# Forward transform: the buffers of its two products and the engine of a 33-row subtraction

## The chip, the cores and the metric

The kernel runs on one core of a Trainium2 chip. A core has TensorE (matrix products into PSUM; PE in the profile, PEld for its weight loads), VectorE (DVE), ScalarE (ACT), GpSimd (POOL) and the queue of SyncE (SP), which issues most transfers. PSUM has eight banks of 512 fp32 values per partition; a product lands in one of them and has to be copied out before the bank can be used again. GpSimd also issues some transfers from its own queue. The metric is the device time of one execution in microseconds (us).

## The reference, cut to what matters

Two independent parts are computed and set side by side. Part A is attention with a compressive memory (32 heads, four segments of 512 positions, projections, output projection). Part B, which the change touches, is a spectral filter:

```python
def _B_ref(x, w_r, w_i):                 # x: 1 x 2048 x 576
    B, S, D = x.shape
    X = jnp.fft.rfft2(x, axes=(-2, -1))  # 2048 x 289, complex
    X = X * (w_r + 1j * w_i)
    return jnp.fft.irfft2(X, s=(S, D), axes=(-2, -1))
...
return jnp.concatenate([a, b], axis=-1)
```

## The kernel before, in words

Part B's forward transform comes first, and the projections of part A follow it. The 2048 rows are split into 16 units of 128 rows. For each unit the transform along the 576 columns is a first product (`f1`) with a table of cosines and sines, and the transform along the 128 rows a second one (`c1`) with a table of its own for each unit (`cfw`). What is left along the 16 units, butterflies and twiddles, is done in place on `Z` (`stage1`, `middle`, `last`), spread over later work by a counter (`pace`) that lets a set number of VectorE instructions go ahead at each place.

fp32 accuracy is had from a fast matmul type by splitting each operand into a rounded high part and the rest (`h` and `l`), and adding three products. So each unit goes through these steps:

- `load`: 384 KB `xin` on SyncE's queue, three buffers.
- `prep`: VectorE makes the sum and the difference of the two mirrored halves (`eo`, two buffers, L125); ScalarE rounds them into `eh` (L127, three buffers); VectorE subtracts to get `el` (L131), and for the rows beyond 256, which lie in partitions 64 to 96 of the third block, subtracts in place in `eh` (L132, 33 rows). Units 0 and 1 do this in halves.
- `f1`: 14 matmuls, seven for the real and seven for the imaginary half, into one PSUM tile of two banks (three such buffers). The seventh of each half reads the 33 rows of L132.
- `ev0` and `ev1`: ScalarE copies the result rounded (`X0`, L146), VectorE subtracts for the rest (`X1`, L149).
- `c1`: 12 matmuls, six for each half, into a one-bank tile for each half (two such buffers).
- `evz`: ScalarE copies either half into `Z` (L153).
- `loadc`: the unit's `cfw` table, issued on GpSimd's queue, four buffers.

The loop over `u` (20 turns) writes the order out by hand, and every engine works its queue in that order: `ev0` of unit u-1, `evz` of unit u-4, the first half of `prep` of unit u+2, `ev1` of unit u-1, one paced step, the second half of `prep`, `f1` of unit u, `load` of unit u+4, `c1` of unit u-3, `loadc` of unit u+1, and one step of splitting part A's weights (`wqkl`, L406 and L407 on VectorE). In the last turns the inputs of the projections are loaded and split instead (L427 to L439). The projections' matmuls are those of L460.

GpSimd has little to do in this stage: a few memsets, three issues for the tables and the sixteen `cfw` issues. Its first subtraction or sum of two tensors is much later, at L532.

Of the kernel before, what the change touches and what calls it, by code (L numbers as in the profile page):

```python
# [5 lines left out]
F32=mybir.dt.float32; F32R=mybir.dt.float32r  # L6
# [96 lines left out]
class FFT:  # L103
# [4 lines left out]
    def forward(s,xp,cp,pp,wl,xs,consts):  # L108

        nc,io=s.nc,s.io; v=nc.vector  # L110
        xin={}; cw={}; C={}; eh={}; el={}; F={}; X={}
        def load(u):
            xin[u]=xp.tile([128,2,3,128],F32,name="xin",bufs=3)
            nc.sync.dma_start(xin[u],io["xb"][u])
        def loadc(u):
            a,b=BORD[u]
            cw[u]=cp.tile([128,2,384],F32R,name="cfw",bufs=4)
            nc.gpsimd.dma_start(cw[u],io["cfw"][4*a+b].rearrange("p (h m) -> p h m",h=2))
        def prep(u,halves=False):

            x=xin.pop(u)
            eo=xp.tile([128,2,3,128],F32,name="eo",bufs=2)
            h=xp.tile([128,2,3,128],F32R,name="eh",bufs=3)
            for r,op in enumerate((OP.add,OP.subtract)):
                v.tensor_tensor(eo[:,r],x[:,0],x[:,1],op=op)  # L125
                if halves: nc.scalar.copy(h[:,r],eo[:,r])
            if not halves: nc.scalar.copy(h,eo)  # L127
            yield
            l=xp.tile([128,2,2,128],F32R,name="el",bufs=3)
            for w in (slice(0,1),slice(1,2)) if halves else (slice(0,2),):  # L130
                v.tensor_tensor(l[:,w],eo[:,w,:2],h[:,w,:2].bitcast(F32),op=OP.subtract)  # L131
                v.tensor_tensor(h[64:97,w,2],eo[64:97,w,2],h[64:97,w,2].bitcast(F32),op=OP.subtract)  # L132
            eh[u],el[u]=h,l
            yield
        def f1(u):
            p=pp.tile([128,2,512],F32,name="f1",tag="f1")
            h,l=eh.pop(u),el.pop(u)
            for r in range(2):
                L=[(h[:,r,0],tab[:,0,r,0]),(h[:,r,1],tab[:,0,r,1]),(h[:,r,0],tab[:,1,r,0]),(h[:,r,1],tab[:,1,r,1]),
                   (l[:,r,0],tab[:,0,r,0]),(l[:,r,1],tab[:,0,r,1]),(h[:99,r,2],tab2[:99,r])]  # L140
                for n,(x,t) in enumerate(L):
                    nc.tensor.matmul(p[:,r,:FP],x,t,start=n==0,stop=n==6)  # L142
            F[u]=p
        def ev0(u):
            x=xp.tile([128,2,FP],F32R,name="X0",bufs=3); X[u]=[x]
            nc.scalar.copy(x,F[u][:,:,:FP])  # L146
        def ev1(u):
            x=xp.tile([128,2,FP],F32R,name="X1",bufs=3)
            v.tensor_tensor(x,F.pop(u)[:,:,:FP],X[u][0].bitcast(F32),op=OP.subtract)  # L149
            X[u].append(x)  # L150
        def evz(u):
            a,b=BORD[u]
            for r,p in enumerate(C.pop(u)): nc.scalar.copy(s.Z[:,b,a,r],p[:,:FP])  # L153
        def c1(u):
            a,b=BORD[u]; x=X.pop(u); cc=cw.pop(u)
            for r in range(2):
                p=pp.tile([128,512],F32,name="c1",tag="c1")
                n=0
                for (i,hl) in ((0,0),(0,1),(1,0)):
                    for q in range(2):  # L160
                        k=(0 if q==0 else 2) if r==0 else (1 if q==0 else 0)
                        nc.tensor.matmul(p[:,:FP],cc[:,hl,k*128:(k+1)*128],x[i][:,q],start=n==0,stop=n==5)
                        n+=1
                C.setdefault(u,[]).append(p)
        load(0)
        tab=cp.tile([128,2,2,2,FP],F32R,name="ftab",bufs=1)
        tab2=cp.tile([128,2,FP],F32R,name="ftab2",bufs=1)
        nc.gpsimd.dma_start(tab[:,0],io["ftab"][:,:4*FP].rearrange("p (r c f) -> p r c f",r=2,c=2))
        late=consts()
        nc.gpsimd.dma_start(tab[:,1],io["ftab"][:,4*FP:].rearrange("p (r c f) -> p r c f",r=2,c=2))  # L170
        nc.gpsimd.dma_start(tab2,io["ftab2"].rearrange("p (r f) -> p r f",r=2))
        load(1); load(2); late()
        for u in range(2): loadc(u)
        p=[prep(u,True) for u in range(2)]
        for i in range(2):
            for x in p: next(x)
        load(3)
        s.pace=Pace(61+165+40)
        for u in range(20):
            p=prep(u+2) if u+2<16 else iter(())  # L180
            if 0<u<17: ev0(u-1)
            if 3<u: evz(u-4)
            if u%4==3 and u>6: s.pace.add(s.stage1((u-7)//4))
            next(p,None)
            if 0<u<17: ev1(u-1)
            if u<14: s.pace.take(1)
            next(p,None)
            if u<16: f1(u)
            if u+4<16: load(u+4)
            elif u<18: next(xs,None)  # L190
            if 2<u<19: c1(u-3)
            if 0<u<15: loadc(u+1)
            if 1<u: next(wl,None)
            if u>13: s.pace.take(2)
        for _ in wl: pass
        for _ in xs: pass
# [188 lines left out]
class ATT:  # L385
# [11 lines left out]
    def consts(s):  # L397
        nc,io=s.nc,s.io
        for i in range(1,4): nc.gpsimd.memset(s.zst[i],0.0)
        return lambda: (nc.sync.dma_start(s.ident,io["ident"]),nc.sync.dma_start(s.bm,io["bm"].rearrange("p (h c) -> p h c",h=7)))  # L400
# [642 lines left out]
def emit(nc,tc,io):  # L1043
    def pool(es,name,bufs=1,**kw):
        return es.enter_context(tc.tile_pool(name=name,bufs=bufs,reuse_waits="tile",**kw))
    with ExitStack() as L0:
        cp=pool(L0,"cp"); dp=pool(L0,"dp",space=bass.MemoryType.DRAM)
        A=ATT(nc,tc,io,cp,dp)
        Rz=ExitStack(); Rv=ExitStack(); Rw=ExitStack(); Ri=ExitStack(); L1x=ExitStack()
        tc.swap_default_side()  # L1050
        zp=pool(Rz,"z"); ftp=pool(Rz,"ft")
        wq=pool(Rw,"wq")
        tc.swap_default_side()
        A.wh,A.wl={},{}
        F=FFT(nc,tc,io,zp); F.tp=A.ftp=ftp
        with tc.manual_schedule():
            x0=pool(L1x,"x0")
            with ExitStack() as es:
                xp=pool(es,"xf",2); cf=pool(es,"cf"); st=pool(es,"st",2)
                pf=es.enter_context(PP(tc,"pf",dict(f1=3,c1=2)))  # L1060
                F.forward(xp,cf,pf,A.load_w("wqk",1152,wq,st,576,"wst",3),A.first(Slots(x0),xp),A.consts)
            with ExitStack() as es:
                wv=pool(Rv,"wv"); xp=pool(es,"xp"); tp=pool(es,"tp",2); fwp=pool(es,"fw",2)
                pp=es.enter_context(PP(tc,"pp",dict(pj=5,pt=1,pm=2)))
                F.pace.add(F.middle(fwp)); F.pace.add(F.last())
                def hook(g,i):
                    if g==3 and i==9:
                        Rw.close()
                        tc.swap_default_side()
                        F.yp=pool(Ri,"yp",2); F.Yt={}; ci=pool(Ri,"ci")  # L1070
                        tc.swap_default_side()
                        F.inv_setup(ci)
                    if g==3 and i>10: F.ysplit(i-11,nc.vector)
                    if g==3 and i==0: q0.extend(A.stacks0(x0))
                    if g==3 and i==3: A.masks()
                    if g==3 and 0<i<7:
                        for _ in range(2): q0.pop(0)()
                q0=[]
                A.projections(xp,tp,pp,wv,F.pace,hook)
            Rv.close()  # L1080
            with ExitStack() as L1:
                cp2=pool(L1,"cp2"); sm=pool(L1,"sm",2); sp=pool(L1,"sp",3)
                ps1=L1.enter_context(PP(tc,"ps1",dict(s1=3)))
                A.begin(sm,sp,ps1)
                with ExitStack() as es:
                    pi=es.enter_context(PP(tc,"pi",dict(i2=2,i3=2,mt=1)))
                    yl=pool(es,"yl",2)
                    A.att_setup(cp2)
                    A.psm,A.mtag=pi,"mt"
                    pr=A.prologue(); next(pr)  # L1090
                    for i,_ in enumerate(F.inverse(yl,pi)):
                        if i>7 and i%4!=3: next(pr,None)
                    for _ in pr: pass
                Ri.close(); Rz.close()
                with ExitStack() as es:
                    tp=pool(es,"tp2",2); ps=es.enter_context(PP(tc,"ps",dict(s2=3,pv=1,post=1)))
                    A.attention(tp,ps)
            L1x.close()
# [18 lines left out]
```

## Time and profile before

| | us |
|---|---|
| median of three runs (725.75 to 726.9) | 725.89 |
| span of the profiled execution, first to last instruction | 725.3 |
| TensorE busy in the span | 693.1 |
| VectorE busy | 551.2 |
| ScalarE busy | 455.1 |
| GpSimd busy | 209.4 |
| first matmul of the forward transform | 8.55 |
| first matmul of the projections | 75.40 |

No other time than the span is given for the profiled execution; the median of the runs lies 0.6 us above it. The granted TensorE clock is 0.999 of full speed over the whole span.

Rows that begin with two numbers are from the order of time: start and duration in us, engine, line, operation, output and inputs with their shapes, count, and in brackets the idle time before and what ended it. Consecutive instructions of the same form are merged into one row; matmuls overlap, so their durations are longer than the distance of their starts. Rows with a bar are groups: count, busy time in us and mean in ns, then the idle time before them. Rows that begin with a stretch (40.00:50.00) give its length, then the busy time and count of TensorE, its weight loads, VectorE, ScalarE and GpSimd, the granted clock, the share of the DMA engines and GB/s. A `q` behind an engine's name marks its instruction queue.

### The profile page before, as it was taken

Reading aid. Unit: us, or ns where it says so; the run is one execution under the profiler, and the core shown is the slowest. Engines: PE = TensorE matmul, PEld = TensorE weight load, DVE = VectorE, ACT = ScalarE, POOL = GpSimd, SP = SyncE. Lnnn points to the kernel's source line nnn. Section 1 sums busy time; section 2 is a strip of 40 time slices with the busy share of each in tenths; the row PEclk is TensorE's granted clock in tenths of the full one; section 3 lists DMA queues with packets and bytes.
Section 4 is the critical chain, followed back from the end, with each engine's and each line's share of the span. In section 5 each row is a group of like instructions: output and inputs, shape, how many; then the busy total and the mean of one; then the engine's idle time right before and its main releaser. Section 6 shows DMA issues by size and latency. Waiting matters only on the chain.

```text
span 725.3 us, 14481 instructions
## 1 busy us (share of the span) xinstructions
PE 693.1 (96%) x5007; PEld 498.8 (69%) x5007; DVE 551.2 (76%) x1281; ACT 455.1 (63%) x1008; POOL 209.4 (29%) x410
## 2 busy tenths in 40 slices
PE   4998999999999999999999999999899999999897
PEld 4988779879779889999844444444565445663397
DVE  6999879899799789787587878877466875667433
ACT  3665796585586574444487777767466776567531
POOL 2111000100200112565065434444142762335310
PEclk9999999999999999999999999999999999999999
DMA  9884435545363668898537656777546675441142
GB/s 339 274 261 156 136 127 183 193 168 177 124 217 131 189 206 275 208 234 224 168 102 185 173 148 146 186 165 159 141 98 172 176 172 133 111 118 41 33 144 84
DMA packets 83245, 121.06 MB, mean 167 GB/s; under 512 B 11352, under 2 KB 50630, under 8 KB 83036
## 3 DMA queue, kind: packets, MB, share of 16 engines
q1 hardware_dynamic: 76580, 104.11, 50.5%
q0 software_dynamic: 6592, 16.03, 7.8%
q8 instruction: 39, 0.64, 0.4%
q14 instruction: 34, 0.28, 0.1%
HBM read 81.78 MB, written 38.24 MB: 165 GB/s over the span
## 4 chain that ended last, share of the span: by engine, by line
PE 76%; DVE 8%; DMA 7%; ACT 5%; issue 3%; POOL 1%; SPq 0%; ACTq 0%; DVEq 0%; POOLq 0%
PE pj L460 14%; PE pv L709 9%; PE s L638 9%; PE pjv L460 8%; PE po L843 7%; PE i L296 4%; PE i L307 4%; PE s L681 3%; PE s L685 2%; PE po L872 2%; DVE eo L125 2%; PE s L690 2%; PE pn L778 2%; PE s L647 2%; PE pm L517 2%
## 5 line engine op out<-in xcount | busy, mean ns | idle before, releaser
L642 DVE CUSTOM_DVE_ANT_0 junk<-s,x 128x512 bf16<-128x512 f32 (+1 forms) x256 | 141.2, 552 | 62.3 <-PE s L638 58.6
L694 POOL TENSOR_SCALAR_AFFINE_SELECT P<-P 128x512 f32<-128x512 f32 x128 | 78.5, 645 | 82.3 <-ACT P L682 74.6
L648 DVE TENSOR_REDUCE mx<-s 128x4 f32<-128x512 f32 x128 | 87.9, 687 | 12.8 <-PE s L647 11.0
L709 PE MATMUL pv<-P,vs 128*32 128x512 f32 (+3 forms) x1024 | 88.8, 442 | 1.0 <-POOL P L694 1.0
L682 ACT ACTIVATE P<-s 128x512 f32<-128x512 f32 x128 | 76.2, 595 | 13.7 <-PE s L681 11.0
L691 ACT ACTIVATE P<-s 128x256 f32<-128x256 f32 x128 | 49.1, 384 | 52.8 <-PE s L690 52.5
L687 ACT ACTIVATE P<-s 128x512 f32<-128x512 f32 x128 | 75.7, 591 | 0.0
L638 PE MATMUL s<-Ks,Qs 108*128 108x384 bf16 (+3 forms) x256 | 69.1, 302 | 1.1 <-DVE mx L648 0.9
L460 PE MATMUL pj<-x,wqkh 128*128 128x512 f32 x162 | 56.5, 409 | 0.0
L638 PEld LDWEIGHTS <-Qs 108*128 108x128 bf16 x320 | 31.6, 99 | 31.5 <-issue 21.9
L206 DVE TENSOR_TENSOR Z<-t,t 128x290 f32<-128x290 f32 (+1 forms) x96 | 48.4, 553 | 0.1
L206 DVE TENSOR_TENSOR t<-Z 128x580 f32<-128x580 f32 x64 | 46.1, 755 | 0.0
L507 POOL MEMSET vt<- 128x32 f32 x16 | 2.3, 161 | 150.5 <-PE pm L517 123.9
L647 PE MATMUL s<-tri,idb 128*128 128x128 bf16 x256 | 43.0, 219 | 0.0
L142 PE MATMUL f<-ftab,eh 128*128 128x290 f32 (+1 forms) x160 | 30.8, 310 | 9.4 <-DMA ftab<-ftab 9.4
L296 PE MATMUL i<-civ,Y 128*128 128x256 f32 (+1 forms) x288 | 39.2, 288 | 0.2 <-POOL Y L281 0.2
L296 PEld LDWEIGHTS i<-civ,Y 128*128 128x128 f32 (+1 forms) x288 | 36.5, 181 | 1.1 <-POOL Y L281 0.4
L709 PEld LDWEIGHTS pv<-P,vs 128*32 128x32 f32 x1024 | 22.1, 108 | 21.9 <-issue 14.5
L307 PE MATMUL i<-itab,T 128*128 128x290 f32 (+1 forms) x224 | 36.3, 305 | 0.1
L460 PE MATMUL pj<-x,wqkl 128*128 128x512 f32 x90 | 35.5, 395 | 0.0
L460 PE MATMUL pj<-xh,wqkl 128*128 128x512 f32 x90 | 35.5, 395 | 0.0
L460 PE MATMUL pj<-xh,wqkh 128*128 128x512 f32 x90 | 35.5, 395 | 0.0
(201 smaller groups left out, 1809.8 us busy)
## 6 DMA issues: line engine op xcount, KB each, us to landing
qkD<-sp SPq DMA_DIRECT2D x36, 384.0 KB
Ks<-qkD SPq DMA_DIRECT2D x72, 144.0 KB
x<-qkD SPq DMA_DIRECT2D x60, 144.0 KB
Qs<-qkD SPq DMA_DIRECT2D x60, 144.0 KB
xin<-xb SPq DMA_DIRECT2D x16, 384.0 KB
cfw<-cfw POOLq DMA_DIRECT2D x16, 384.0 KB, 4.5
civ<-civ POOLq DMA_DIRECT2D x16, 384.0 KB, 7.4
vs<-vD SPq DMA_DIRECT2D x16, 330.0 KB
```

Of the source, the lines that this page charges most:

```text
L206: v.tensor_tensor(o,a,b,op=op)
L296: nc.tensor.matmul(p[:m,k],Y[i][:,q,c*128:c*128+m],cc[:,hl,o:o+256],start=n==0,stop=n==5)
L307: nc.tensor.matmul(p,x,t,start=n==0,stop=n==6)
L460: s.nc.tensor.matmul(out,a,b,start=i==0,stop=i==len(L)-1)
L638: nc.tensor.matmul(out,Q[:108,h,128*i:128*i+128],K[:108,h,:128*(i+1)],start=True,stop=True)
L642: nc.vector.tensor_tensor_reduce(out=junk[:,:w],in0=src,in1=s.mask[:,512-w:],scale=1.0,scalar=-3.0e38, op0=OP.add,op1=OP.max,accum_out=s.m ...
L647: nc.tensor.matmul(pa[:,o+w-128:o+w],s.idb,s.tri,start=False,stop=True,skip_group_check=True)
L648: nc.vector.tensor_reduce(out=s.mx[k][:,hh],in_=pa.rearrange("p (b c) -> p b c",c=128),axis=mybir.AxisListType.X,op=OP.max)
L682: nc.scalar.activation(P[0][:,hh],p0,AF.Exp,scale=SC)
L687: nc.scalar.activation(P[1][:,hh],p1,AF.Exp,scale=SC)
L694: nc.gpsimd.affine_select(out=x,in_=x,pattern=pat+[[1,128]],compare_op=OP.is_ge,fill=0.0,base=0,channel_multiplier=-1)
L709: nc.tensor.matmul(s.pvt[32*hh:32*hh+32,128*j:],vt[:,j,19*h:19*h+32],mv[0][:,hh,mv[1]],start=j==0,stop=j==2,skip_group_check=True)
```

## The change

Three edits in the forward transform.

- The in-place subtraction on 33 rows (L132) is issued on GpSimd instead of VectorE, for all units.
- The second product's two halves go into one tile of two banks instead of two tiles of one, and `evz` copies both halves with a single ScalarE instruction.
- The first product has two buffers of two banks instead of three; the second has two buffers of two banks instead of two of one. Eight banks are used before and after.

```diff
-                v.tensor_tensor(h[64:97,w,2],eo[64:97,w,2],h[64:97,w,2].bitcast(F32),op=OP.subtract)
+                nc.gpsimd.tensor_tensor(h[64:97,w,2],eo[64:97,w,2],h[64:97,w,2].bitcast(F32),op=OP.subtract)
...
         def evz(u):
             a,b=BORD[u]
-            for r,p in enumerate(C.pop(u)): nc.scalar.copy(s.Z[:,b,a,r],p[:,:FP])
+            nc.scalar.copy(s.Z[:,b,a],C.pop(u)[:,:,:FP])
         def c1(u):
             a,b=BORD[u]; x=X.pop(u); cc=cw.pop(u)
+            p=C[u]=pp.tile([128,2,512],F32,name="c1",tag="c1")
             for r in range(2):
-                p=pp.tile([128,512],F32,name="c1",tag="c1")
                 n=0
...
-                        nc.tensor.matmul(p[:,:FP],cc[:,hl,k*128:(k+1)*128],x[i][:,q],start=n==0,stop=n==5)
+                        nc.tensor.matmul(p[:,r,:FP],cc[:,hl,k*128:(k+1)*128],x[i][:,q],start=n==0,stop=n==5)
                         n+=1
-                C.setdefault(u,[]).append(p)
...
-                pf=es.enter_context(PP(tc,"pf",dict(f1=3,c1=2)))
+                pf=es.enter_context(PP(tc,"pf",dict(f1=2,c1=2)))
```

## The prediction

> **What bounds the kernel now.** The change lies in the forward transform, the first 75 us, so I read the stretches first (busy time of each engine by window, then granted clock, share of the DMA engines, GB/s), then the order of time, then the waits.
>
> ```profile
> span 725.3 us, 14481 instructions
> 0.00:10.00 10.00, 0.82 (x2) 0.50 (x2) 5.80 (x14) 3.29 (x6) 4.67 (x14) 1.00 0.87 292
> 10.00:20.00 10.00, 9.75 (x60) 9.64 (x61) 7.21 (x13) 4.28 (x6) 0.00 (x0) 1.00 1.04 371
> 40.00:50.00 10.00, 9.03 (x63) 8.32 (x62) 9.84 (x18) 6.87 (x15) 1.47 (x3) 1.00 0.87 270
> ```
>
> From 40 to 50 us VectorE (third engine column) is busy 9.84 of 10 us and TensorE only 9.03: VectorE sets the pace there. The order of time shows one turn of the loop:
>
> ```profile
> 46.66 1.02 DVE L125 TENSOR_TENSOR eo<-xin 128x384 f32<-128x384 f32 x2
> 47.60 0.76 DVE L149 TENSOR_TENSOR X<-f,X 128x580 fp32r<-128x580 f32 x1
> 48.27 0.75 DVE L206 TENSOR_TENSOR t<-Z 128x580 f32<-128x580 f32 x1
> 48.94 0.68 DVE L131 TENSOR_TENSOR el<-eo,eh 128x512 fp32r<-128x512 f32 x1
> 49.66 0.42 DVE L132 TENSOR_TENSOR eh<-eo,eh 33x256 fp32r<-33x256 f32 x1
> 50.08 1.88 PE L162 MATMUL c<-X,cfw 128*128 128x290 f32 x12 [0.34 <-ACT Z L153]
> 50.11 0.76 DVE L406 TENSOR_TENSOR wqkl<-raw,wqkh 128x576 fp32r<-128x576 f32 x1
> 50.79 1.02 DVE L125 TENSOR_TENSOR eo<-xin 128x384 f32<-128x384 f32 x2
> ```
>
> VectorE runs from the sums of one unit (46.66) to the next (50.79) without a gap: 4.13 us a turn. The instruction that the change moves is L132: from the start of `el` to the start of `wqkl` 1.17 us pass. TensorE's second product (L162) meanwhile waits 0.34 us for ScalarE's copy of the previous one; between 20 and 70 us that is 3.7 us in seven waits:
>
> ```profile
> PE c L162 <- ACT Z L153: 3.7, 7, 1.2
> 20.89 0.70 PE L142 MATMUL f<-ftab,eh 128*128 128x290 f32 x4
> 22.79 1.02 DVE L125 TENSOR_TENSOR eo<-xin 128x384 f32<-128x384 f32 x2
> 24.41 0.70 PE L142 MATMUL f<-ftab,eh 128*128 128x290 f32 x4
> 26.31 1.78 PE L162 MATMUL c<-X,cfw 128*128 128x290 f32 x12
> 27.93 0.69 PE L142 MATMUL f<-ftab,eh 128*128 128x290 f32 x4
> 64.62 0.76 DVE L149 TENSOR_TENSOR X<-f,X 128x580 fp32r<-128x580 f32 x1
> ```
>
> The starts at 24.41, 26.31 and 27.93 give TensorE's own price of a turn without waits: 1.90 us for the 14 matmuls of the first product, 1.62 for the 12 of the second, 3.52 together. So VectorE costs up to 0.6 us a turn. Its ten full turns (units 4 to 13 of the loop) run from the sums at 22.79 to L149 at 64.62.
>
> **The change part by part.**
>
> *The low part off VectorE.* The nearest rows are of a late stage, where VectorE and GpSimd run side by side, and of GpSimd's own prices:
>
> ```profile
> 662.68 0.69 DVE L826 TENSOR_TENSOR am<-ux,am 126x512 f32<-126x512 f32 x1
> 663.29 1.12 DVE L813 TENSOR_TENSOR ol<-am,oh 126x512 fp32r<-126x512 f32 x1
> 668.09 0.68 DVE L813 TENSOR_TENSOR ol<-am,oh 126x512 fp32r<-126x512 f32 x1
> 663.13 2.95 POOL L694 TENSOR_SCALAR_AFFINE_SELECT P<-P 128x512 f32<-128x512 f32 x4 [0.53 <-ACT P L682]
> 191.93 0.82 DVE L206 TENSOR_TENSOR t<-Z 128x580 f32<-128x580 f32 x1
> L739 POOL TENSOR_TENSOR ry<-ry,rw 128x128 f32<-128x128 f32 x8 | 3.4, 429 | 23.0 <-ACT rw L738 22.9
> L281 POOL TENSOR_TENSOR Y<-Z,Y 128x512 fp32r<-128x512 f32 x14 | 17.0, 1214 | 24.2 <-ACT Y L280 22.2 <-DVE T L328 1.9
> ```
>
> Without L132 `wqkl` follows `el` at once, as 663.29 follows 662.68 (same width): 0.61 us instead of 1.17, so 0.56 a turn less, and a turn of 3.57 us. Against it stands that the moved instruction on GpSimd reads the same memory at the same moment. The same subtraction L813 takes 0.68 us alone and 1.12 when GpSimd had begun a 128x512 instruction 0.16 us before it: VectorE with two operands in SBUF stands still for 0.44 us although it had been running back to back, so GpSimd gets its turn between two of VectorE's instructions. At 191.93 the loss was 0.07 (0.82 against 0.75 of the same form at 48.27), behind a smaller one. GpSimd's own price for the 256 elements is between 0.43 (128 elements) and 1.21 (512), on the line 0.69. The low part waits for the same cast of `eh` as `el` does, and `el`, `wqkl` and the sums all take both operands from SBUF, so it must meet one of them each turn. Bounds of the loss: 0.07 and the whole 0.69; I take 0.45, the row at 663.29, since that is the one with VectorE running back to back on both sides. Then a turn is 4.02 us, 0.11 shorter, over the ten turns: **-1.1 us**. The Trainium skill ("SBUF — State Buffer", Who interferes with whom) says that VectorE with two SBUF inputs and a GpSimd instruction that reads SBUF exclude each other for a whole instruction; by that rule, with which the 1.12 us agree, the gain is the small one.
>
> *The start.* GpSimd's queue holds one thing more:
>
> ```profile
> L532 POOLq MODIFY_POOL_CONFIG  x2: 7/9/11, 179.3 to 179.4; - x2
> 190.03 0.44 POOL L532 TENSOR_TENSOR Mst<-mm,Mst 126x126 f32<-126x126 f32 x1 [10.62 <-DVE mm L525]
> 3.65 2.14 POOL L118 DMA_DIRECT2D cfw<-cfw  x4
> 8.88 1.03 DVE L125 TENSOR_TENSOR eo<-xin 128x384 f32<-128x384 f32 x2
> 13.30 1.03 DVE L125 TENSOR_TENSOR eo<-xin 128x384 f32<-128x384 f32 x2 [1.34 <-DMA xin<-xb]
> 16.46 1.03 DVE L125 TENSOR_TENSOR eo<-xin 128x384 f32<-128x384 f32 x2
> 18.45 0.69 DVE L131 TENSOR_TENSOR el<-eo,eh 128x512 fp32r<-128x512 f32 x1 [0.28 <-ACT eh L127]
> 19.63 1.03 DVE L125 TENSOR_TENSOR eo<-xin 128x384 f32<-128x384 f32 x2
> 182.00:186.00 4.00, 4.00 (x24) 3.46 (x23) 1.83 (x4) 1.88 (x6) 0.00 (x0) 1.00 0.46 141
> ```
>
> Ahead of GpSimd's first TENSOR_TENSOR of the program, and nowhere else, a pair of MODIFY_POOL_CONFIG stands in its queue. Before, that is at 179.3 us, and whatever it starts is hidden: the instruction waits until 190.03 for VectorE anyway. With the change the first TENSOR_TENSOR is the low part of unit 0, right behind two `cfw` issues, at 3.65 + 2 x 0.535 = 4.72 us. Its duration is not shown; bounds are 0 and the 10.6 us of that wait. I take 9.0, towards the upper row, because at the start the DMA engines are at a share of 0.87 and 1.04, and 0.46 from 182 to 186, and code that has to be fetched will be slower there.
>
> Who waits: `eo` has two buffers, so VectorE's sums for unit 2 wait until GpSimd has read `eo` of unit 0, two low parts of 0.4 us after the load; behind these sums in VectorE's queue stands everything. Step by step: 4.72 + 9.0 + 0.83 + 0.05 = 14.60 for the sums of unit 2 (8.88 before); from there to `el` 1.99, as from 16.46 to 18.45, and 0.35 for unit 1's two small low parts, which they meet; from `el` to the next sums 0.61 + 0.45: the sums of unit 3 at 18.0, where 13.30 (a wait for a load) stood. Three turns later they were at 22.79, 9.49 after 13.30; now from `el` to the sums it is 1.06 for 1.18 (18.45 to 19.63), 9.13 in all, so 27.1: **+4.3 us**. The cover that went is the wait until 13.30, 4.4 us of slack after 8.88; a load under 4.7 us would cost nothing here. The `cfw` issues of units 2 and 3 now stand behind low parts, from 4.7 to about 21 us; their product is then due at about 31, so they cost nothing, and they take load off the first 10 us. The first product's last matmul per half needs the low part too, but VectorE is later than that.
>
> *The buffers of the products.* The first goes from three buffers to two, the second from two single banks to two pairs.
>
> ```profile
> 65.03 0.69 PE L142 MATMUL f<-ftab,eh 128*128 128x290 f32 x4
> 75.40 0.63 PE L460 MATMUL pj<-x,wqkh 128*128 128x512 f32 x2
> L153 ACT COPY Z<-c 128x290 f32<-128x290 f32 x32 | 11.5, 407 | 2.0 <-PE c L162 2.0
> L146 ACT CAST X<-f 128x580 fp32r<-128x580 f32 x16 | 10.2, 638 | 5.9 <-PE f L142 3.3 <-PE c L162 2.6
> ```
>
> The second product of a unit no longer needs the copy of the unit just before, but the one before that, a turn older: its waits (3.7 us to 70 us) go, though in the turns VectorE sets the time and only TensorE's idle place moves: the first product now waits for VectorE's L149 of two units back, about 1.75 us into VectorE's turn. That queues nothing late, for 3.52 us of matmuls fit into 4.02. At the end it counts: after the last low part VectorE is free and TensorE has its last first product and four second ones left. Before, L149 of unit 13 started at 64.62 and the projections at 75.40, 10.78 us. After: 0.80 for that L149, then 1.90 + 4 x 1.62 = 8.38 without waits, 9.2 us: **-1.6 us**. One copy of 580 for two of 290 costs ScalarE about 0.64 (the cast of that form) where the pair took 0.70 from start to end (each 0.41, overlapped); ScalarE idles before each cast of `eh`, so zero.
>
> *Sum.* -1.1 + 4.3 - 1.6 = +1.6 us on a span of 725.3: 726.9. The median of the runs, 725.89, is 0.6 above the span, so **727.5 us**. From 75 us on I let the shift run through unchanged, since TensorE is then nearly always busy.
>
> **The rivals.** About 0.2%, 1.45 us, is what a measurement of this kernel can tell from no change.
>
> (a) *The load is short.* If it ends well before 13 us, the slack after 8.88 hides most of it. Each us less than 9.0 gives a us back down to 4.7: with 6 us the sum is -1.4, 724.5; with none it is -0.36 for the start and -3.1 in all, 722.8. For: the row at 179.3 shows only a ceiling. Against: the traffic of the start. The Trainium skill ("GPSIMD Engine Reference", Instruction dispatch) gives 5.95 us for the first call of a freshly loaded kernel; by that figure the estimate is 724.4, and no row here shows its length.
>
> (b) *GpSimd yields to VectorE* (the other sign). If the low part costs VectorE 0.07 instead of 0.45, its turn is 3.64, about TensorE's 3.52, and TensorE becomes the bound: with the load at 9.0 the first product of unit 4 starts at about 25.0 us (20.9 before), the one of unit 15 11 x 3.52 later at 63.7, the projections 8.4 later at 72.1 instead of 75.40: 722.6. For: 191.93 with its 0.07. Against: 663.29. It decides from a loss under about 0.2 us a turn.
>
> (c) *Both are dear.* 0.69 a turn adds 2.4 us, a load of 11 adds 2.0: 731.9. For: a two-operand instruction on GpSimd takes longer than the one-operand one at 663.13.
>
> (d) *The saving is taken back in the projections.* If ScalarE rather than TensorE sets the time between 90 and 110 us, the 1.6 us of the tail are lost: 729.1.
>
> **How the numbers follow.** My forecast's case (load 8 to 10.6, loss 0.4 to 0.55) gets 0.47, its own range 726.0 to 730.1; (a) 0.28, half of it within 0.2%; (b) 0.11; (c) 0.09; (d) 0.05. The forecast's case lies to about a quarter within 0.2%. So faster 0.28, within 0.2% 0.26, slower 0.46. The range reaches from (b) and the unhidden rest of (a) at 722.5 to 730.8; left out are loads above 11 us with the full loss.
>
> **What would show it.** In the changed profile: MODIFY_POOL_CONFIG near 4.7 us and GpSimd's first TENSOR_TENSOR near 13.7 (if near 10.7, (a)); VectorE's second pair of sums at about 14.6, with a wait for GpSimd; `el`, `wqkl` or the sums 0.45 us longer once a turn and a turn of about 4.0 us (if 3.5 to 3.65, (b); if over 4.2, (c)); no waits of L162 for L153; the projections starting at 77.0. The prediction is wrong if GpSimd needs no load there, or if VectorE's instructions keep their durations.

## The result, and the profile after

The changed kernel takes 723.62 us (median of 18 runs) where the kernel before took 725.87 on the same chip (also 18): a ratio of 0.9971, with a 95% interval of 0.9959 to 0.9983. It is faster by 0.29%, about 2.1 us. The forecast was 727.5 us, slower.

From the page of the changed kernel and from its table of busy time by stretch (columns as before):

```profile
span 719.9 us, 14480 instructions
...
0.00:10.00 10.00, 1.64 (x5) 1.31 (x6) 5.30 (x10) 3.78 (x6) 6.09 (x16) 1.00 0.86 301
10.00:20.00 10.00, 9.70 (x54) 9.38 (x53) 7.64 (x12) 3.71 (x7) 4.76 (x5) 1.00 0.98 337
40.00:50.00 10.00, 9.37 (x68) 8.89 (x67) 10.00 (x15) 6.10 (x11) 3.88 (x6) 1.00 0.89 261
```

This profile is of a run of 721.65 us, the fastest of the 18; the 5.4 us between the two spans are therefore not what the change is worth. 2.8 of them lie behind the start of the projections, outside the stage that was changed (725.3 - 75.40 against 719.9 - 72.83). From 40 to 50 us VectorE, which gave an instruction away, is busy all 10.00 us. The order of time shows the start and a turn:

```profile
5.39 2.48 POOL L132 TENSOR_TENSOR eh<-eo,eh 33x128 fp32r<-33x128 f32 x4 [0.66 <-ACT eh L126]
8.42 1.01 DVE L125 TENSOR_TENSOR eo<-xin 128x384 f32<-128x384 f32 x2
12.51 1.03 DVE L125 TENSOR_TENSOR eo<-xin 128x384 f32<-128x384 f32 x2 [1.48 <-DMA xin<-xb]
...
41.61 1.02 DVE L125 TENSOR_TENSOR eo<-xin 128x384 f32<-128x384 f32 x2
42.55 0.75 DVE L149 TENSOR_TENSOR X<-f,X 128x580 fp32r<-128x580 f32 x1
43.22 0.75 DVE L205 TENSOR_TENSOR t<-Z 128x580 f32<-128x580 f32 x1
43.64 0.93 POOL L132 TENSOR_TENSOR eh<-eo,eh 33x256 fp32r<-33x256 f32 x1 [2.65 <-ACT eh L127]
43.89 1.23 DVE L131 TENSOR_TENSOR el<-eo,eh 128x512 fp32r<-128x512 f32 x1
45.04 0.75 DVE L405 TENSOR_TENSOR wqkl<-raw,wqkh 128x576 fp32r<-128x576 f32 x1
...
63.55 0.76 DVE L149 TENSOR_TENSOR X<-f,X 128x580 fp32r<-128x580 f32 x1
64.37 0.80 PE L142 MATMUL f<-ftab,eh 128*128 128x290 f32 x4
72.83 0.63 PE L459 MATMUL pj<-x,wqkh 128*128 128x512 f32 x2
```

- The start isn't late: GpSimd's first low part runs at 5.39 us, and VectorE's sums of unit 2 start at 8.42 (8.88 before).
- `el` takes 1.23 us where it took 0.68, so `wqkl` follows 1.15 us after its start; before, with L132 between the two, it was 1.17. From sums to sums a turn takes 4.09 us (41.61 to 45.70, the next such row).
- From L149 of unit 13 to the projections 9.28 us pass (63.55 to 72.83); before, 10.78.

The list of waits from the start to 76 us (total in us, times, longest) had TensorE's second product, L162, wait for ScalarE's copy, L153, before; that wait is gone. After, the first product waits for VectorE's L149 in its place:

```profile
PE c L162 <- ACT Z L153: 4.4, 8, 1.2
```
```profile
PE f L142 <- DVE X L149: 2.5, 5, 1.2
```

What GpSimd's queue holds ahead of its first low part, from the rows of L132 in the changed kernel:

```profile
L132 POOLq MODIFY_POOL_CONFIG  x2: 77/77/77, 4.7 to 4.7; - x2
```

### The profile page after: what moved, and what is told of

Same layout as the page of the kernel before. It is cut to its first block, busy times and chain, and to the rows that moved or that the text cites. A ratio compares the mean times of both kernels' runs of the same rounds, so it can differ in the third digit from the quotient of the medians.

```text
span 719.9 us, 14480 instructions
## 1 busy us (share of the span) xinstructions
PE 693.1 (96%) x5007; PEld 500.1 (69%) x5007; DVE 550.2 (76%) x1263; ACT 453.7 (63%) x992; POOL 226.9 (32%) x428
## 4 chain that ended last, share of the span: by engine, by line
PE 71%; DMA 6%; ACT 4%; DVE 3%; issue 2%; POOL 1%; SPq 0%; ACTq 0%; DVEq 0%; POOLq 0%
PE pj L459 12%; PE pv L708 9%; PE s L637 9%; PE po L842 7%; PE pjv L459 7%; PE i L306 4%; PE i L295 4%; PE s L680 3%; PE s L684 2%; PE po L871 2%; PE s L689 2%; PE pn L777 2%; PE s L646 2%; PE pm L516 2%; DMA ux<-uD 1%
## 5 line engine op out<-in xcount | busy, mean ns | idle before, releaser
L637 PE MATMUL s<-Ks,Qs 108*128 108x384 bf16 (+3 forms) x256 | 69.1, 302 | 1.1 <-DVE mx L647 0.9
L205 DVE TENSOR_TENSOR Z<-t,t 128x290 f32<-128x290 f32 (+1 forms) x96 | 48.4, 554 | 0.1
L205 DVE TENSOR_TENSOR t<-Z 128x580 f32<-128x580 f32 x64 | 46.1, 755 | 0.0
L142 PE MATMUL f<-ftab,eh 128*128 128x290 f32 (+1 forms) x160 | 32.5, 323 | 11.1 <-DMA ftab<-ftab 8.7
```

Source lines behind the costliest of these rows:

```text
L205: v.tensor_tensor(o,a,b,op=op)
L637: nc.tensor.matmul(out,Q[:108,h,128*i:128*i+128],K[:108,h,:128*(i+1)],start=True,stop=True)
```

## The experiments

One thing has to be known to compare starts. The transform can't go ahead before the second half of its table (`ftab`) has landed, and that moves between profiles: the second pair of L142's matmuls, which waits for it, started at 10.25 us before and 9.19 after, and between 9.26 and 11.17 in the experiments.

```profile
10.25 0.85 PE L142 MATMUL f<-ftab,eh 128*128 128x290 f32 x2 [0.87 <-DMA ftab<-ftab]
```
```profile
9.19 0.85 PE L142 MATMUL f<-ftab,eh 128*128 128x290 f32 x2 [0.87 <-DMA ftab<-ftab]
```

The 11.17 is of a kernel (e4 below) whose program up to there is that of the changed kernel with its 9.19. So I give the start of the projections as its distance from that start: before 75.40 - 10.25 = 65.15, after 72.83 - 9.19 = 63.64. There is one profile of each kernel, and the distance scatters too: in e5 below, whose stage is that of the kernel before, it is 65.87. TensorE also runs its first matmuls at about six a us and gets to nine or ten at a point that moves, between 13 and 19 us in these profiles, though the granted clock is given as 1.00 throughout. Differences of 0.7 us and less are not read from this distance.

Theory 1 (the forecast): the load of GpSimd's code costs at the start, the buffers save at the end, the move saves a little in each turn. Theory 2: there is no load, the move saves nothing since `el` loses what L132 cost, and the buffers alone are the gain.

**Either part alone.** The first kernel has only the move to GpSimd, the second only the buffers with the single copy:

```diff
 # e1_low_only: the kernel before, with
-                v.tensor_tensor(h[64:97,w,2],eo[64:97,w,2],h[64:97,w,2].bitcast(F32),op=OP.subtract)
+                nc.gpsimd.tensor_tensor(h[64:97,w,2],eo[64:97,w,2],h[64:97,w,2].bitcast(F32),op=OP.subtract)
 # e2_buffers_only: the changed kernel, with the same line back on VectorE
-                nc.gpsimd.tensor_tensor(h[64:97,w,2],eo[64:97,w,2],h[64:97,w,2].bitcast(F32),op=OP.subtract)
+                v.tensor_tensor(h[64:97,w,2],eo[64:97,w,2],h[64:97,w,2].bitcast(F32),op=OP.subtract)
```

> Only the low part goes to GpSimd; the buffers stay as before. Theory: the move itself brings almost nothing in the ten full turns, because each low part on GpSimd holds up one VectorE instruction by about 0.54 us, as much as it saves; a turn of VectorE stays at 4.1 us, TensorE keeps its waits for ScalarE's copy (L153), the end from L149 of unit 13 to the projections stays at about 10.8 us. The start is 1.3 us earlier. Projections at about 74.1, time 1.0 to 1.3 us under before (about 724.8). Rival, the move is the whole gain: projections at 72.8, time as with the full change.

> Only the buffers and the single copy; L132 stays on VectorE. Theory: a turn stays at 4.13 us, the waits for L153 vanish, the end from L149 of unit 13 to the projections goes from 10.8 to 9.3 us, the start is as before: projections at 73.9, time about 1.5 us under before (724.4). Rival, the move is the whole gain: projections at 75.4, time as before.

Measured: the move alone 726.69 us against 726.29, ratio 0.9999 (0.9987 to 1.0012); the buffers alone 724.12, ratio 0.9971 (0.9955 to 0.9987), the same as both together. The projections start 64.9 and 63.5 us behind the landing (65.15 before, 63.64 after). I had expected something of the move, because VectorE's start was 1.3 us earlier in the changed kernel (the sums of unit 6 at 21.46 against 22.79); with the move alone they are at 22.51, and the changed kernel's landing was 1.06 us earlier than before. From the move's order of time and its list of waits:

```profile
44.92 1.23 DVE L131 TENSOR_TENSOR el<-eo,eh 128x512 fp32r<-128x512 f32 x1
46.07 0.75 DVE L406 TENSOR_TENSOR wqkl<-raw,wqkh 128x576 fp32r<-128x576 f32 x1
```
```profile
PE c L162 <- ACT Z L153: 4.3, 8, 1.2
```

and from the order of time of the buffers alone:

```profile
65.19 0.76 DVE L149 TENSOR_TENSOR X<-f,X 128x580 fp32r<-128x580 f32 x1
74.46 0.63 PE L459 MATMUL pj<-x,wqkh 128*128 128x512 f32 x2
```

With the move alone `el` is stretched just as in the changed kernel and the waits of L162 for L153 are all there (4.3 us in eight, 4.4 before). With the buffers alone the end takes 9.27 us, as after. From the landing to L149 of unit 13 pass 54.4 us before and after (64.62 - 10.25, 63.55 - 9.19). So the gain is the buffers', and 1.5 us of it are seen at the end of the stage; the other 0.6 us of the measured 2.1 lie within its interval. The move is worth nothing that the runs can tell: its interval reaches about 0.9 us to either side. The buffers and the single copy were not tried apart.

**The low part left out.** This kernel is the changed one without the line of the low part: the 33 partitions then hold the rounded values a second time where the rest should be, so the output is wrong, but all other work is left.

```diff
-                nc.gpsimd.tensor_tensor(h[64:97,w,2],eo[64:97,w,2],h[64:97,w,2].bitcast(F32),op=OP.subtract)
```

> The changed kernel with the 33-row subtraction left out altogether (so these rows of the low part are missing from the transform): the move as it would be if it cost VectorE nothing. Theory: no instruction of VectorE is stretched, a turn falls to 3.5 to 3.6 us, where TensorE's matmuls set it, projections at 67.5 to 69, time 719 to 720.5. Rival, GpSimd is not what holds VectorE up and the turn has another bound: projections at about 72.8, time as with the full change.

Measured: 718.44 us, ratio 0.9900 (0.9883 to 0.9917); the projections 58.2 us behind the landing. The order of time of VectorE:

```profile
41.57 1.02 DVE L125 TENSOR_TENSOR eo<-xin 128x384 f32<-128x384 f32 x2
...
43.85 0.68 DVE L131 TENSOR_TENSOR el<-eo,eh 128x512 fp32r<-128x512 f32 x1
44.46 0.75 DVE L404 TENSOR_TENSOR wqkl<-raw,wqkh 128x576 fp32r<-128x576 f32 x1
45.13 1.02 DVE L125 TENSOR_TENSOR eo<-xin 128x384 f32<-128x384 f32 x2
```

The turn is 3.56 us: VectorE still runs without a gap, and hardly slower than TensorE's price (3.52). A GpSimd instruction that no engine is seen to wait for costs the kernel 0.7% (0.9971 against 0.9900). In the stage it does so through the 0.53 to 0.55 us that it adds to one VectorE instruction of each turn: `el` in most, the sums in the first turns (1.56 us for 1.03, at 15.14 in the changed kernel) and `wqkl` in some (1.29 us at 52.69).

**What is shared?** One kernel does the GpSimd subtraction twice; the other leaves the low part out and has GpSimd write, for about as long, without reading:

```diff
 # e6_low_twice: the changed kernel, behind the low part
+                sc=xp.tile([128,2,128],F32,name="sc",bufs=1)
+                nc.gpsimd.tensor_tensor(sc[64:97,w],eo[64:97,w,2],eo[64:97,w,2],op=OP.subtract)
 # e7_write_only: the changed kernel, in place of the low part
-                nc.gpsimd.tensor_tensor(h[64:97,w,2],eo[64:97,w,2],h[64:97,w,2].bitcast(F32),op=OP.subtract)
+                sc=xp.tile([128,640],F32,name="sc",bufs=1)
+                for _ in range(2): nc.gpsimd.memset(sc[64:97],0.0)
```

> The changed kernel with a second GpSimd subtraction of the same size behind each low part, into a tile that nobody reads. Theory (each GpSimd instruction that reads SBUF holds up one VectorE instruction for its own reading time): a turn goes from 4.10 to about 4.6 us, two instructions of VectorE stretched by about 0.54 us each, projections about 5 us later than with the full change. Rival (VectorE is stretched by a wait for the low part's result, or by the first one only): turn 4.10 as before.

> The changed kernel with the low part left out (its rows are missing from the transform) and in its place two GpSimd memsets of 33x640, which write SBUF and read nothing. Theory (what VectorE shares with GpSimd is the reading of a second operand): no instruction of VectorE is stretched, a turn of 3.5 to 3.6 us as without any low part. Rival (any use of SBUF by GpSimd holds VectorE up): instructions stretched, a turn of 4.0 us or more.

Measured in one run each, beside a median of 726.28 for the kernel before: 727.64 and 719.31 us; the projections 69.1 and 58.7 us behind the landing. The orders of time, first with the second subtraction (L134):

```profile
42.66 0.93 POOL L132 TENSOR_TENSOR eh<-eo,eh 33x256 fp32r<-33x256 f32 x1 [2.05 <-ACT eh L127]
42.91 1.23 DVE L131 TENSOR_TENSOR el<-eo,eh 128x512 fp32r<-128x512 f32 x1
43.56 1.05 POOL L134 TENSOR_TENSOR sc<-eo 33x256 f32<-33x256 f32 x1
44.06 1.17 DVE L407 TENSOR_TENSOR wqkl<-raw,wqkh 128x576 fp32r<-128x576 f32 x1
45.15 1.01 DVE L125 TENSOR_TENSOR eo<-xin 128x384 f32<-128x384 f32 x2
```

then with writes alone:

```profile
41.39 1.34 POOL L133 MEMSET sc<- 33x640 f32 x2
42.48 0.69 DVE L131 TENSOR_TENSOR el<-eo,eh 128x512 fp32r<-128x512 f32 x1
43.08 0.75 DVE L406 TENSOR_TENSOR wqkl<-raw,wqkh 128x576 fp32r<-128x576 f32 x1
```

The second subtraction stretches a second VectorE instruction, `wqkl`, by 0.42 us, and the turn goes from 4.09 to 4.52 (40.63 to 45.15), a little less than expected. `wqkl` shares no tile with either subtraction, so it isn't a wait for their results. The two memsets lie beside a step of L206 and end at 42.73, beside `el`, and stretch nothing; the turn is 3.55. So it isn't that GpSimd works, and not that it writes: it is its reading of SBUF while VectorE reads two operands there. The Trainium skill ("SBUF — State Buffer", Who interferes with whom) says just this, that such a VectorE instruction contends with a GpSimd instruction that reads SBUF and not with one that only writes it; these two runs agree.

**Another place for the low part.** Of VectorE's instructions in a turn only L149 has an operand in PSUM. In the first of these kernels the paced step goes ahead of L149, so that ScalarE's cast, and with it the low part, comes while L149 runs; in the second the weights' split too, whose cast and subtraction become two steps:

```diff
 # e4_step_first: the changed kernel, with the two lines exchanged
             next(p,None)
-            if 0<u<17: ev1(u-1)
             if u<14: s.pace.take(1)
+            if 0<u<17: ev1(u-1)
             next(p,None)
...
 # e9_weights_between: the same, and the weights' subtraction between the two
             if u<14: s.pace.take(1)
+            if 2<u: next(wl,None)
+            if 0<u<17: ev1(u-1)
...
-    def wsplit(s,nm,x,t,o,w):
+    def wsplit(s,nm,x,t,o,w,two=False):
...
+        def d():
+            nc.vector.tensor_tensor(l[:m],x[:m],h[:m].bitcast(F32),op=OP.subtract)
...
+        if two: return d
+        d()
...
-                s.wsplit(nm,x,t,o,w)
+                d=s.wsplit(nm,x,t,o,w,two)
+                if two:
+                    yield
+                    d()
```

> The changed kernel with the paced VectorE step ahead of L149 instead of behind it. L149 has one operand in PSUM, and the low part then falls into it. Theory (VectorE and GpSimd shut each other out only where both read SBUF with VectorE's two operands): the loss falls from 0.54 to about 0.2 us in the turns with a paced step (units 7 to 13), a turn from 4.10 to about 3.75, projections at about 70.4, time about 2.3 us under the full change (721.3). Rival, the loss only moves to the next instruction: turn 4.10, projections at 72.8 or, as L149 comes later, up to 73.5.

> The changed kernel with another order on VectorE: sums, paced step, subtraction of the weights (L405, its ScalarE cast stays where it was), then L149, then el. The low part is ready while the paced step or the weights run and gets its turn at the end of one of them, and what follows then is L149 with one operand in PSUM. Theory: nothing of VectorE is stretched in the turns with a paced step, a turn of 3.55 to 3.65 us, projections about 4 us earlier than with the full change at the same arrival of the table, time about 719.5. Rival (GpSimd takes its turn ahead of the weights or of el): one stretched instruction a turn, 3.9 to 4.1 us, time 722 to 723.5.

Measured: 723.54 us, ratio 0.9962 (0.9949 to 0.9976) for the first; 720.81 us against 726.28, ratio 0.9934 (0.9914 to 0.9953) for the second. The projections start 63.0 and 60.1 us behind the landing. The order of time of the first:

```profile
41.08 0.74 DVE L149 TENSOR_TENSOR X<-f,X 128x580 fp32r<-128x580 f32 x1
41.49 0.73 POOL L132 TENSOR_TENSOR eh<-eo,eh 33x256 fp32r<-33x256 f32 x1 [2.65 <-ACT eh L127]
41.75 1.02 DVE L131 TENSOR_TENSOR el<-eo,eh 128x512 fp32r<-128x512 f32 x1
```

and of the second:

```profile
31.95 1.56 DVE L125 TENSOR_TENSOR eo<-xin 128x384 f32<-128x384 f32 x2
...
39.66 1.02 DVE L125 TENSOR_TENSOR eo<-xin 128x384 f32<-128x384 f32 x2
40.59 0.76 DVE L206 TENSOR_TENSOR t<-Z 128x580 f32<-128x580 f32 x1
41.27 0.75 DVE L407 TENSOR_TENSOR wqkl<-raw,wqkh 128x576 fp32r<-128x576 f32 x1
41.93 0.74 POOL L132 TENSOR_TENSOR eh<-eo,eh 33x256 fp32r<-33x256 f32 x1 [0.96 <-ACT eh L127]
41.94 0.75 DVE L149 TENSOR_TENSOR X<-f,X 128x580 fp32r<-128x580 f32 x1
42.61 0.68 DVE L131 TENSOR_TENSOR el<-eo,eh 128x512 fp32r<-128x512 f32 x1
43.21 1.02 DVE L125 TENSOR_TENSOR eo<-xin 128x384 f32<-128x384 f32 x2
```

In the first the low part starts 0.41 us after L149 and outlasts it by 0.40 us; `el` loses 0.34 of that, not the 0.2 that I expected, and the turn is 3.90 us, not 3.75. Its time can't be told from the changed kernel's; 721.3 was expected. In the second the low part lies wholly beside L149, takes its undisturbed 0.74 us, `el` its 0.68, and the turn is 3.55. That is the version that beats both kernels: its interval ends at 0.9953, that of the changed kernel begins at 0.9959, so the two do not overlap. It falls short of the kernel without the low part (58.2 behind the landing) by 1.9 us. Most of that is lost in the early turns, where the low part still meets the sums, as at 31.95: by the sums that start at 36.11, and at 34.47 without the low part, it is 1.8 us behind, counted from the landing.

**The load of code alone.** The kernel before, with one GpSimd subtraction in front of everything, on a buffer that nobody reads:

```diff
         load(0)
+        dm=xp.tile([128,128],F32,name="dm",bufs=1)
+        nc.gpsimd.memset(dm,0.0)
+        nc.gpsimd.tensor_tensor(dm[64:97],dm[64:97],dm[64:97],op=OP.subtract)
```

> The kernel before with one extra GpSimd subtraction of two tensors (33x128, its operands just set by GpSimd itself) at the very start of its queue, so that its first TENSOR_TENSOR has nothing to wait for. It measures what MODIFY_POOL_CONFIG starts. Theory, from the changed profile, where the first low part came 0.7 us behind it: the gap from MODIFY_POOL_CONFIG to the subtraction is under 0.7 us. Rival, a load of 6 to 9 us that the changed kernel somehow hid: a gap of several us, and the first table transfers issued that much later.

Measured: 726.1 us in one run, beside a median of 726.28. The rows of the added line, and GpSimd's order of time:

```profile
L168 POOLq MODIFY_POOL_CONFIG  x2: 11/11/11, 1.0 to 1.0; - x2
```
```profile
0.81 0.20 POOL L167 MEMSET dm<- 128x128 f32 x1 [0.29 <-POOLq L1107]
1.10 0.40 POOL L168 TENSOR_TENSOR dm<-dm 33x128 f32<-33x128 f32 x1
1.46 0.73 POOL L171 DMA_DIRECT2D ftab<-ftab  x1
```

From MODIFY_POOL_CONFIG to the end of the first TENSOR_TENSOR 0.5 us pass, 0.40 of them the instruction itself. No load is to be seen. In the changed kernel MODIFY_POOL_CONFIG stands at 4.7 us and the first low part at 5.39, after a wait of 0.66 us for ScalarE's cast. The figure of about 6 us in the Trainium skill ("GPSIMD Engine Reference", Instruction dispatch) doesn't appear in either.

## Why the prediction was wrong

- **The start (+4.3 us): this step failed.** The forecast took 9.0 us for what MODIFY_POOL_CONFIG starts, out of bounds of 0 and 10.6, and the lower bound was the true one: 0.1 us until the next instruction. The row at 190.03 showed a wait for VectorE, with no part of it that had to be a load; traffic at the start was an argument for a duration that nothing had shown. Any load under 4.7 us of those 10.6 would have cost nothing here, by the forecast's own working, and rival (a), which holds these cases, got only 0.28. The measured 723.62 us lies between the ends that the forecast gave, 722.5 and 730.8, only because (a) and (b) were counted in. (By the cases' own chances, faster adds up to 0.25 and slower to 0.49, not 0.28 and 0.46.)
- **The low part off VectorE (-1.1 us): right mechanism, mis-sized.** The exclusion is there and was read from the right row (663.29). The loss was taken as 0.45 us and measured 0.55 (1.23 for 0.68), as much as the 0.56 that the move saves. A turn of 4.09 us instead of 4.02, and of 4.13 before: the term is next to nil, as the ratio 0.9999 of the move alone agrees. Here the low part, started at 43.64 beside L205, which lasts until 43.97, takes 0.20 us more than its undisturbed 0.73 and holds up the instruction behind, not the one that it meets first. The rows also show why 663.29 lost less: in each of them VectorE loses what GpSimd's instruction still has to run when VectorE's one before ends, less 0.05 or 0.06 us. For `el` that is 0.60 us (43.97 to 44.57, loss 0.55), at 663.29 0.50 (663.37 to 663.87, where the first of the four at 663.13 ends; loss 0.44), for `wqkl` behind the second subtraction 0.47 (44.14 to 44.61, loss 0.42), in the kernel with the step moved ahead 0.40 (41.82 to 42.22, loss 0.34). The row at 191.93, on which rival (b) rested, lost only 0.07 because GpSimd's instruction, begun at 191.71, was nearly done (192.13, VectorE free at 192.01); GpSimd didn't yield there.
- **The buffers (-1.6 us): right.** The waits of L162 for L153 went, the first product waits for L149 instead without cost that shows, and the end took 9.28 us where 9.2 was forecast: -1.50. With the buffers alone it was 9.27. The single copy, put at zero, was not tried apart; no wait of L162 for it shows.
- **The sum.** With 0 for the start and 0 for the move, the forecast's own third term gives 725.89 - 1.6 = 724.3, within the measured interval of -1.2 to -3.0 us. Rival (a) with no load, 722.8, had the direction and the mechanism right, and the same error of 0.1 us a turn. Rival (b), GpSimd yields, didn't happen, but its sum was near: with no loss VectorE and TensorE are about even, both busy for 10.00 of the 10 us from 40 to 50 in the kernel without the low part, with a turn of 3.56 us.
- **The base.** I took 0.6 us, median less span, for what lies outside the span. It is 1.7 to 1.8 us (721.65 against 719.9 after); by that, the profile of before was of a run some 1 us slower than the median. This didn't move the forecast, which starts from the median, but the marks of one profile scatter by as much as the terms of the sum.

## What to carry to other kernels

Moving an instruction from VectorE to an idle GpSimd gained nothing here, since its operands are in SBUF and VectorE runs one two-operand instruction after another there: the time comes back in VectorE's next row. Compare what VectorE saves (0.56 us here) with what GpSimd will still have to run when VectorE's instruction ends (0.60). Look for a VectorE instruction with a PSUM operand and make the moved one ready just as that begins. A cost at a program's start that no row shows is to be held against the slack there before it is made the main term, and starts are compared from the last input that they wait for.

## What the runs showed of the hardware

- A GpSimd subtraction of 33x256 (0.73 us undisturbed) delays a back-to-back VectorE instruction with two SBUF operands by 0.53 to 0.55 us where it becomes ready beside another such instruction, and a second subtraction delays the next one by 0.42. The delay is what GpSimd has left when VectorE's instruction before ends, less 0.05 or 0.06 us (0.60 us left and 0.55 lost; 0.50 and 0.44; 0.47 and 0.42; 0.40 and 0.34; 0.12 and 0.07). GpSimd gets its turn between two of VectorE's instructions, though VectorE is never idle; it then takes 0.92 us and more itself.
- VectorE's L149, with one operand in PSUM, took its 0.75 us with the low part wholly beside it (0.74), so neither lost anything.
- GpSimd's memsets of 33x640 (0.67 us each) delayed nothing on VectorE.
- GpSimd's first TENSOR_TENSOR of the program started about 0.1 us after MODIFY_POOL_CONFIG.
- The landing of the table's second half moves by 2.0 us between the profiles (9.19 to 11.17 us), and with it the stage behind it.
